# Two groups of weight sums moved to VectorE and the next batch's x sums moved one quad later, in a fused FFT mixing and ELU feed-forward kernel

## The chip, the cores and the metric

The kernel runs on one core of a Trainium2 chip. The metric is the time of one execution in microseconds (us) on the device; lower is better. A core has TensorE (PE, matrix multiply), VectorE (DVE), ScalarE (ACT), GpSimd (POOL) and SyncE (SP). In this kernel SP does nothing but issue DMA transfers, one after the other; a few transfers are issued by POOL and ACT. Each engine runs its own instructions in program order and waits on semaphores of the others.

## The reference

Two stages, all in float32. The first multiplies each of 8 sequences of length 3008 (256 channels) by a filter in the frequency domain; the second is a feed-forward block with an ELU between two matrix products.

```python
X = np.fft.rfft(x, axis=1)                 # x: (8, 3008, 256)
F = (filt_r + 1j * filt_i)[None, :, :]     # 1505 frequencies x 256
y = np.fft.irfft(X * F, n=3008, axis=1)
h = y.reshape(24064, 256) @ w_in           # 256 x 2048
g = np.where(h > 0.0, h, np.exp(np.minimum(h, 0.0)) - 1.0)
out = g @ w_out                            # 2048 x 256
```

## The kernel before

**The transform.** 3008 is 47 x 64. Each of the 8 batches goes through a transform along 64 (a_unit on PE, from x sums made by x_unit on DVE), a transform along 47 with the filter between (b_unit, then the products and sums re_mult, re_sums, im_mult, im_join, im_sums on DVE, then bi_unit), and a transform back along 64 (n_unit). Between these steps the data goes through DRAM to change its layout: z_write and z_read between a_unit and b_unit, y_write and y_read between bi_unit and n_unit. For the first batch there are separate functions (names with `_first`) that run in a prologue.

**The feed-forward block.** The result of n_unit for a batch and a sixth m (448 tokens for m=0, 512 for the others) is the input of four items q = 0 to 3, one for each quarter of the 2048 hidden columns. Both products use a Strassen scheme with seven products in place of eight, so for each item there are seven "up" steps (w_in) and seven "down" steps (w_out), each of four matmuls. An up step's result is kept by ACT (`keep`, L552) or added by DVE (`add`, L549); the ELU takes two ACT operations (`elu_exp`, L558 and L559) and one of DVE (`elu_max`, L563), and four more DVE operations make the combinations for the down steps (L599 to L603). The scheme also needs sums of pieces of the weights: `w_sums(k)` makes four of them, each 128x256, for piece k. The 16 weight pieces arrive as float64 and are converted on the chip: `w_split` (DVE), `w_float` (four ACT operations), `w_join` (DVE), then `w_sums` for every second piece.

**Quads.** The main loop (L977) runs over quads: quad i holds the seven up steps of item i and the seven down steps of item i-1, interleaved in a fixed order. For i from 0 on, item i is (b, m, q) in order, six times four items, so 24 quads, to a batch. All other work is put into a plan, `plan[(quad, place)]`, a list of functions for four places in a quad: places 2 and 3 come after the third and fifth step of the first half, place 0 in the middle, place 1 at the end of the quad. A list is run in the order in which `at(quad, place, fn, ...)` filled it:

```python
for fn, a in plan.get((i, 0), ()):
    fn(*a)
```

The table of the weight pieces fills it first, then f_pairs and the clearings, then the loop `for b in range(B)` with everything of batch 0, then everything of batch 1, and so on. In the loop for batch b, t is (b-1)*24. The order inside a quad, and the position of each engine's and each queue's instructions, follows from this alone; there is no other scheduler.

The quads of batch 0 up to quad 7 in the profiled execution, by the start of their first step on PE:

| quad | starts at (us) | what stands at its end on PE before the change |
|---|---|---|
| 0 | 87.0 | |
| 1 | 94.3 | n_unit(0,1), 106.03 |
| 2 | 107.8 | a_unit(1,0), 124.14 |
| 3 | 126.6 | a_unit(1,2), 137.44 |
| 4 | 139.3 | a_unit(1,4), 150.86 |
| 5 | 152.8 | n_unit(0,2), 164.94 |
| 6 | 166.7 | b_unit(1,0), 178.91 |
| 7 | 183.2 | |

**SP's queue.** x_load(b, c) issues seven transfers (one of the table ta, six of x), z_write(b, c) two (L308), z_read(b, g) four (L314), tn_read and y_read one each (L471, L477), f_pairs(c, u) three or four (L775 to L779), y_write four, and o_unit the out writes of a sixth, 24 for m=0 (L672, the DVE part being two adds and the transposes at L662). x_load for chunk c+4 can only start when a_unit has freed the buffer of chunk c.

**Where POOL works.** POOL issues the filter reads (f_read, L324), and before the change makes the sums of pieces 7, 11 and 13 (L750) and clears two filter buffers (L933).

Of the kernel before, what the change touches and what calls it, by code (L numbers as in the profile page):

```python
# [131 lines left out]
def kernel(  # L132
# [9 lines left out]
    nc = tc.nc  # L142
# [34 lines left out]
    fbufs = [fall[:, i] for i in range(FBUFS)]  # L177
# [502 lines left out]
    def w_fetch(k, queue=nc.gpsimd):  # L680
        q, j = divmod(k, 4)

        if k in (3, 4, 14, 15):
            wd = t2[:, k % 11 - 3].rearrange("p u d -> p (u d)")
        elif k == 10:
            wd = t1p.tile([P, XC, D], FP32, tag="t1", name="wd").rearrange("p u d -> p (u d)")
        elif k in (6, 7, 8, 9):
            wd = xp.tile([P, 2, 2, D], FP32, tag="xc", name="wd").rearrange("p k u d -> p (k u d)")
        else:
            wd = fbufs[{5: 0, 11: 0, 12: 1, 13: 2}.get(k, k)].rearrange("p c u d -> p (c u d)")  # L690
        wd = wds[k] = wd.bitcast(U32).rearrange("p (a w) -> p a w", w=2)
        if j < 2:
            srcs = [moe_w_in.bitcast(U32)[ts(j, P), ts(q, 1024)]]
        else:
            srcs = [moe_w_out.bitcast(U32)[ts(4 * q + 2 * (j - 2) + i, P), :] for i in range(2)]
        for i, s in enumerate(srcs):
            n = 512 // len(srcs)
            queue.dma_start(wd[:, ts(i, n), :].rearrange("p a w -> p (a w)"), s)
# [6 lines left out]
    def w_split(k):  # L705
        m, e, f, l = wts[k] = wtmp[{9: 2, 10: 1, 11: 0, 12: 3, 13: 4, 15: 5}.get(k, k % 2)]
        hi = wds[k][:, :, 1]
        nc.vector.tensor_scalar(out=m, in0=hi, scalar1=0x000FFFFF, scalar2=None, op0=ALU.bitwise_and)
        nc.vector.tensor_scalar(out=e, in0=hi, scalar1=0x7FF00000, scalar2=None, op0=ALU.bitwise_and)

    def w_float(k, *parts):
        m, e, f, l = wts[k]
        ef = e.bitcast(FP32)
        steps = ((l, wds[k][:, :, 0], AXT.Identity, 2.0 ** -52, 0.0), (f, m, AXT.Identity, 2.0 ** -20, 1.0),
                 (ef, e, AXT.Relu, -8.0, edges[:, 0:1]), (e, ef, AXT.Relu, -1.0, edges[:, 1:2]))
        for i in parts or range(4):
            o, x, func, scale, bias = steps[i]
            nc.scalar.activation(out=o, in_=x, func=func, scale=scale, bias=bias)

    def w_join(k, parts=(0, 1)):  # L720
        q, j = divmod(k, 4)
        m, e, f, l = wts[k]
        if 0 in parts:
            nc.vector.scalar_tensor_tensor(out=e, in0=wds.pop(k)[:, :, 1], scalar=0x80000000, in1=e,
                                           op0=ALU.bitwise_and, op1=ALU.bitwise_or)
            nc.vector.tensor_tensor(out=f, in0=f, in1=l, op=ALU.add)
        if 1 not in parts:
            return
        e = e.bitcast(FP32)
        if j < 2:  # L730
            f, e = (t.rearrange("p (a j c) -> p a j c", a=2, j=2) for t in (f, e))
            dst = w_in[q][:, 2 * j:2 * j + 2, :, :].rearrange("p j a c -> p a j c")
            nc.vector.tensor_tensor(out=dst, in0=f, in1=e, op=ALU.mult)
        else:

            f, e = (t.rearrange("p (i a e s) -> p i e a s", i=2, a=4, e=2) for t in (f, e))
            dst = w_out[q][:, 0:4, j - 2, :].rearrange("p (i e) (a s) -> p i e a s", i=2, a=4)
            for i in range(2):
                nc.vector.tensor_tensor(out=dst[:, i], in0=f[:, i], in1=e[:, i], op=ALU.mult)
        if j % 2 == 1 and k < 7:  # L740
            w_sums(k)

    def w_sums(k, engine=nc.vector, parts=(0, 1, 2, 3)):
        q, j = divmod(k, 4)
        w = (w_in if j < 2 else w_out)[q]
        a11, a21, a12, a22, s1, s2, s4 = (w[:, i] for i in range(7))
        sums = ((s1, a21, a22, ALU.add), (s2, s1, a11, ALU.subtract), (s4, a12, s2, ALU.subtract), (a21, a11, a21, ALU.subtract))
        for i in parts:
            o, x, y, op = sums[i]
            engine.tensor_tensor(out=o, in0=x, in1=y, op=op)  # L750
# [30 lines left out]
    with tc.manual_schedule():  # L781


        with tc.tile_pool(name="boot", bufs=1) as bp:
# [68 lines left out]
            c = t1p.tile([P, XC, D], FP32, tag="t1", name="wfl").rearrange("p (a b) d -> p a (b d)", a=2)  # L853
            places(c[:, 0], flat(tnp.tile([P, 4, P], FP32, tag="tn", name="we")), c)
            for t in (zq, rq):
                t = t.rearrange("p a u d -> p a (u d)")
                places(t[:, 0], t[:, 1], t[:, 2:4])
            t = t3f.rearrange("p a (b u) d -> p (a b) (u d)", u=2)
# [1 line left out]
            w_split(7)  # L860
            w_join(6)
            w_split(8)
            floats = {0: (7, 0, 1), 1: (7, 2, 3), 2: (8, 0, 1), 3: (8, 2, 3), 4: (9, 0, 1), 5: (9, 2, 3), 6: (10, 0, 1), 7: (10, 2, 3)}
            for g in range(4):
                t_first(g)
            for g in range(NG + 2):
# [20 lines left out]
            y_read(0, 0, slice(0, K2 - 4), slice(K2 - 4, K2))  # L887
            for k in (14, 15):
                w_fetch(k, nc.sync)
            w_join(8)  # L890
            for k in (11, 12, 13):
                w_split(k)
# [2 lines left out]
            w_sums(9)  # L895
            w_join(10)
            w_join(11)
            w_sums(11, nc.gpsimd)
            warm = psO.tile([P, 512], FP32, tag="po2", name="warm")
            for k in range(7):  # L900
                nc.tensor.matmul(warm, w_in[0][:, 0, 0, :], w_in[0][:, 0:2].rearrange("p a b c -> p (a b c)"),
# [15 lines left out]
        def at(quad, place, fn, *a):  # L917
            plan.setdefault((quad, place), []).append((fn, a))


        for quad, place, fn, *a in ((0, 0, w_split, 14), (1, 2, w_join, 12), (1, 2, w_split, 15), (1, 2, w_float, 14, 0, 1),
                                    (1, 3, w_float, 14, 2, 3), (2, 2, w_float, 15, 0, 1), (2, 3, w_float, 15, 2, 3),
                                    (2, 0, w_join, 14, (0,)), (2, 1, w_join, 14, (1,)), (2, 1, w_join, 15),
                                    (3, 0, w_sums, 15, nc.vector, (0, 1, 2)), (3, 1, w_sums, 15, nc.vector, (3,))):
            at(quad, place, fn, *a)
        for c in range(2, XBUFS):
# [3 lines left out]
            for u in range(2):  # L930
                at(1 + 2 * c + u, 0, f_pairs, c, u)
        for i in range(2):
            at(2 + i, 1, nc.gpsimd.memset, fbufs[i], 0.0)  # L933
        for b in range(B):
            t = (b - 1) * PER
            if b > 0:
                for c, s in enumerate((2, 2, 3, 3, 4, 4) if b == 1 else (0, 0, 3, 3, 4, 4)):
                    at(t + s, 0, x_unit, b, c)
                    if c % 2 == 0:
                        opens.add(t + s + 1)  # L940
                        at(t + s, 1, a_unit, b, c)
                    nb, nxt = (b, c + XBUFS) if c + XBUFS < NXC else (b + 1, c + XBUFS - NXC)
                    if nb < B:
                        at(t + s, 1, x_load, nb, nxt)
                    at(t + s, 1, z_write, b, c)
                for g in range(0, NG, 2):
                    s = t + 6 + 2 * g
                    opens.update((s + 1, s + 4))
                    for k in (g, g + 1):
                        at(s - 2, 1, f_read, b, k)  # L950
                        at(s - 1, 0, z_read, b, k)
                    at(s, 1, b_unit, b, g)
                    at(s + 1, 2, re_mult, b, g)
                    at(s + 1, 1, re_sums, b, g)
                    parts = ((0, 0), (0, 1), (1, 0), (1, 1))
                    early = 3 if g == 6 else 4
                    at(s + 2, 2, im_mult, b, g, *parts[:early])
                    at(s + 2, 1, im_mult, b, g, *parts[early:])
                    at(s + 2, 1, im_join, b, g)
                    at(s + 3, 2, im_sums, b, g)  # L960
                    at(s + 3, 1, bi_unit, b, g)
                    at(s + 3, 1, y_write, b, g)
            for m, (s, place) in enumerate(((23, 0), (25, 1), (29, 1), (32, 0), (36, 0), (40, 0))):
                if b > 0 or m > 0:
                    at(t + s - 2, 0, tn_read, b, m)
                    at(t + s - 2, 1 if m == 0 else 0, y_read, b, m)
                    at(t + s, place, n_unit, b, m)

                    at(*((t + s + 1, 1) if m > 2 else (t + s, place)), n_sums, b, m)
                if b == 0 and m == 1:  # L970
                    at(1, 1, w_join, 13)
                    at(1, 1, w_sums, 13, nc.gpsimd)
                at(t + PER + 4 * m + 5, 0, c_unit, b, m)
                at(t + PER + 4 * m + 6, 0, o_unit, b, m)

        items = [(b, m, q) for b in range(B) for m in range(6) for q in range(4)]
        for i in range(-PER, len(items) + 3):  # L977
# [3 lines left out]
            for n, k in enumerate("DUUDUDDU" if i in opens else "UUDUDDU"):  # L981
                s = ups if k == "U" else downs
# [7 lines left out]
            for k in "DUUDUD" if i in opens else "DUUDUDD":  # L990
                s = ups if k == "U" else downs
# [40 lines left out]
```

## Time and profile before

Three executions took 2587.74, 2592.74 and 2596.02 us; the median is 2592.74. The profiled execution took 2593.74 us, of which the span of the instructions is 2591.9.

| | |
|---|---|
| median of three executions | 2592.74 us |
| profiled execution, its span | 2593.74 us, 2591.9 us |
| PE busy | 2551.7 us, 98% of the span |
| DVE busy | 2041.2 us, 79% |
| ACT busy | 1548.1 us, 60% |
| POOL busy | 169.1 us, 7% |
| mean granted clock of PE | 0.993 |

How to read the lines. A timeline line has the start, the time (of one instruction or, merged, of a run of them), engine, source line, operation, the tile written and the tiles read, the shape, and in brackets how long the engine had been idle before and what ended that. SPq is SP's sequencer, which issues transfers. A line of waits names the engine and line that waited, what it waited for, and the total, the count and the longest wait in us. A row of a stretch (`A:B`) has its length, the busy time of PE, PE's weight loads, DVE, ACT and POOL with instruction counts, the granted clock of PE as a share of full speed, the busy share of the DMA engines, and GB/s.

### The profile page before, as it was taken

The page shows a single profiled execution, that of the slowest core. Times are in us where ns is not written, and L with a number is a line of the kernel's source. Part 1 is how long each engine was busy: PE and PEld are TensorE (multiplying, and loading weights), DVE is VectorE, ACT ScalarE, POOL GpSimd, SP SyncE. Part 2 cuts the span into 40 slices and gives each one's busy share as a digit, 9 for nine tenths or more (in the row PEclk, how much of TensorE's full clock was granted, in tenths as well). Part 3 has the DMA queues.
Part 4 walks back from the last instruction along what each step waited for, and adds up shares of the span by engine and source line. Part 5 has one row for each costly group of instructions (what it writes and reads, how often), then busy time and mean ns, then how long its engine had stood idle before and what let it go on. Part 6 is the DMA issues. An engine that isn't in the chain of part 4 may idle for free.

```text
span 2591.9 us, 39471 instructions
## 1 busy us (share of the span) xinstructions
PE 2551.7 (98%) x14474; PEld 2204.0 (85%) x14474; DVE 2041.2 (79%) x3524; ACT 1548.1 (60%) x2713; POOL 169.1 (7%) x325
## 2 busy tenths in 40 slices
PE   6899999999999999999999999999999999999998
PEld 4688889888898888988889888888889888898887
DVE  6868887788877888788886888778887788866666
ACT  6755556656566655665556656566655655555554
POOL 5100100010000000000000000000000010000000
PEclk8999999999999999999999999999999999999999
DMA  9662213422234231433215231243213322110010
GB/s 282 169 184 69 70 36 88 129 70 63 51 100 108 61 78 42 119 81 76 62 44 151 63 84 37 78 122 84 61 43 87 91 60 68 37 49 20 21 29 17
DMA packets 229177, 206.35 MB, mean 80 GB/s; under 512 B 128666, under 2 KB 195418, under 8 KB 228984
## 3 DMA queue, kind: packets, MB, share of 16 engines
q1 hardware_dynamic: 213624, 172.94, 26.2%
q0 software_dynamic: 14000, 30.44, 4.3%
q8 instruction: 114, 1.87, 0.3%
q10 hardware_dynamic: 1360, 0.46, 0.1%
q14 instruction: 79, 0.65, 0.1%
HBM read 131.87 MB, written 78.17 MB: 81 GB/s over the span
## 4 chain that ended last, share of the span: by engine, by line
PE 96%; DMA 2%; DVE 1%; ACT 0%; issue 0%; SPq 0%; DVEq 0%; ACTq 0%
PE po L623 44%; PE phs L541 25%; PE phd L541 13%; PE pha L541 6%; PE psn L490 3%; PE psa L234 2%; PE pf L383 2%; PE pv L455 1%; DMA xc<-in_x_dram 1%; DMA x<-in_x_dram 0%; PE po L330 0%; DMA yd<-t 0%; PE po L296 0%; PE psr L330 0%; DMA t<-yd 0%
## 5 line engine op out<-in xcount | busy, mean ns | idle before, releaser
L623 PE MATMUL po<-g,wo 128*128 128x256 f32 (+1 forms) x5376 | 1315.1, 377 | 0.0
L623 PEld LDWEIGHTS po<-g,wo 128*128 128x128 f32 x5376 | 1013.6, 190 | 163.6 <-issue 49.7
L552 ACT ACTIVATE g<-phs 128x512 f32<-128x512 f32 (+1 forms) x576 | 339.0, 589 | 751.6 <-PE phs L541 750.2
L559 ACT ACTIVATE e<-e 128x512 f32<-128x512 f32 (+1 forms) x768 | 477.2, 621 | 24.4
L549 DVE TENSOR_TENSOR g<-phd,g 128x512 f32<-128x512 f32 (+1 forms) x384 | 259.6, 676 | 293.6 <-ACT e L559 205.1
L541 PE MATMUL phs<-ys,wi 128*128 128x256 f32 (+1 forms) x1536 | 387.6, 375 | 2.0 <-ACT g L552 1.5
L541 PE MATMUL phs<-y,wi 128*128 128x256 f32 (+1 forms) x1536 | 388.5, 375 | 0.0
L563 DVE SCALAR_TENSOR_TENSOR g<-e,g 128x512 f32<-128x512 f32 (+1 forms) x576 | 387.3, 672 | 0.3 <-ACT e L559 0.2
L558 ACT ACTIVATE e<-g 128x512 f32<-128x512 f32 (+1 forms) x576 | 353.4, 614 | 46.7 <-DVE g L549 38.1
L541 PEld LDWEIGHTS phs<-ys,wi 128*128 128x128 f32 x1536 | 291.4, 190 | 36.0 <-ACT g L552 3.0
L541 PEld LDWEIGHTS phs<-y,wi 128*128 128x128 f32 x1536 | 288.2, 190 | 35.8 <-ACT g L552 0.2
L563 DVE SCALAR_TENSOR_TENSOR g<-e,phs 128x512 f32<-128x512 f32 (+1 forms) x192 | 130.0, 677 | 140.3 <-ACT e L559 139.9
L541 PE MATMUL phd<-ys,wi 128*128 128x256 f32 (+1 forms) x768 | 196.2, 378 | 3.1 <-DVE g L549 3.1
L541 PE MATMUL pha<-y,wi 128*128 128x256 f32 (+1 forms) x768 | 194.0, 375 | 0.0
L541 PE MATMUL phd<-y,wi 128*128 128x256 f32 (+1 forms) x768 | 193.7, 375 | 0.0
L558 ACT ACTIVATE e<-phs 128x512 f32<-128x512 f32 (+1 forms) x192 | 113.0, 589 | 128.7 <-PE phs L541 128.7
L541 PEld LDWEIGHTS phd<-ys,wi 128*128 128x128 f32 x768 | 145.0, 191 | 24.1 <-DVE g L549 8.2
L541 PEld LDWEIGHTS pha<-y,wi 128*128 128x128 f32 x768 | 145.6, 190 | 17.5 <-ACT y L492 0.2
L541 PEld LDWEIGHTS phd<-y,wi 128*128 128x128 f32 x768 | 145.8, 190 | 16.5
L324 POOL DMA_DIRECT2D fall<-fp x224 | 110.5, 501 | 733.4 <-DVE r L428 704.3
L549 DVE TENSOR_TENSOR g<-pha,g 128x512 f32<-128x512 f32 (+1 forms) x192 | 129.3, 673 | 25.9 <-PE pha L541 25.7
L600 DVE TENSOR_TENSOR g<-g,g 128x512 f32<-128x512 f32 (+1 forms) x192 | 130.7, 681 | 6.6
(155 smaller groups left out, 2097.8 us busy)
## 6 DMA issues: line engine op xcount, KB each, us to landing
yd<-t SPq DMA_DIRECT2D x127, 192.0 KB
t<-yd SPq DMA_DIRECT2D x47, 512.0 KB
z<-t SPq DMA_DIRECT2D x84, 256.0 KB
fall<-fp POOLq DMA_DIRECT2D x224, 96.0 KB, 3.0
t<-z SPq DMA_DIRECT2D x224, 96.0 KB
out_dram<-o SPq DMA_DIRECT2D x632, 32.0 KB
tn<-tn_t SPq DMA_DIRECT2D x48, 256.0 KB
xc<-in_x_dram SPq DMA_DIRECT2D x84, 128.0 KB
```

Of the source, the lines that this page charges most:

```text
L234: nc.tensor.matmul(p[o:o + 64, u, :], w[r, u, o:o + 64], src[r, u, :], start=True, stop=True)
L324: nc.gpsimd.dma_start(t[32 * a:32 * a + 24].rearrange("p c u d -> p (c u d)"), fp[g, a].rearrange("q c u d -> q (c u d)"))
L383: nc.tensor.matmul(pf[p][1][32 * a:32 * a + 32, js, :], fb[r, v, :], t2[r, js, a, :], start=True, stop=True, tile_position=(32 * p, 32 * a))
L490: nc.tensor.matmul(ps[:, ts(q, P)], t[:, i - 4 * m, ds(dh * P, P)], w[:, i - 4 * m, :], start=True, stop=True)
L541: nc.tensor.matmul(ps[:, a, 0:h], w_in[q][:, COMBO[n], a, :], y[n], start=start and a == 0, stop=True, skip_group_check=True)
L549: nc.vector.tensor_tensor(out=g[o], in0=i0, in1=i1, op=ALU.add)
L552: nc.scalar.activation(out=g[o], in_=i0, func=AXT.Copy)
L558: nc.scalar.activation(out=e, in_=src, func=AXT.Relu, scale=-1.0)
L559: nc.scalar.activation(out=e, in_=e, func=AXT.Exp, scale=-1.0)
L563: nc.vector.scalar_tensor_tensor(out=g[n], in0=es[n], scalar=1.0, in1=src, op0=ALU.subtract, op1=ALU.max)
L600: nc.vector.tensor_tensor(out=b12, in0=b22, in1=b12, op=ALU.subtract)
L623: nc.tensor.matmul(po[i][:, u, 0:h], w_out[q][:, COMBO[n], a, :], g[n][:, a, :], start=q == 0 and a == 0 and n in (1, 3, 6, 4), stop=True, ...
```

## The change

Seven small edits of the plan and of the prologue:

- The last two conversions of piece 10 are issued after the loop over the spectrum groups, no longer in its group 7.
- The four sums of piece 11 move from POOL, at the prologue's end, to DVE in the middle of quad 0, behind `w_split(14)`.
- The four sums of piece 13 move from POOL, at the end of quad 1, to DVE in quad 2, place 2. The first part of `w_join(14)` moves from the middle of quad 2 to place 2 as well, behind these sums.
- The clearings of the two filter buffers move from POOL (ends of quads 2 and 3) to ACT (both in quad 3, places 2 and 3).
- For batch 1 the x sums, with a_unit, the x loads and the z writes behind them, move from quads 2, 3 and 4 to quads 3, 4 and 5. The quads whose order of steps opens with a down step move along.
- The z reads of batch 1, g = 0 and 1, move from the middle of quad 5 to the middle of quad 6.
- n_unit(0,2) moves from the end of quad 5 to the middle of quad 4, with its tn and y reads from quad 3 to quad 2; its sums stay at the end of quad 5.

In the list of (quad 6, place 0) the out writes and the reads of batch 0 are entered in the loop's turn for b = 0, the z reads in its turn for b = 1.

```diff
--- before.py
+++ after.py
@@ -860,7 +860,7 @@
             w_split(7)
             w_join(6)
             w_split(8)
-            floats = {0: (7, 0, 1), 1: (7, 2, 3), 2: (8, 0, 1), 3: (8, 2, 3), 4: (9, 0, 1), 5: (9, 2, 3), 6: (10, 0, 1), 7: (10, 2, 3)}
+            floats = {0: (7, 0, 1), 1: (7, 2, 3), 2: (8, 0, 1), 3: (8, 2, 3), 4: (9, 0, 1), 5: (9, 2, 3), 6: (10, 0, 1)}
             for g in range(4):
                 t_first(g)
             for g in range(NG + 2):
@@ -887,6 +887,7 @@
             y_read(0, 0, slice(0, K2 - 4), slice(K2 - 4, K2))
             for k in (14, 15):
                 w_fetch(k, nc.sync)
+            w_float(10, 2, 3)
             w_join(8)
             for k in (11, 12, 13):
                 w_split(k)
@@ -895,7 +896,6 @@
             w_sums(9)
             w_join(10)
             w_join(11)
-            w_sums(11, nc.gpsimd)
             warm = psO.tile([P, 512], FP32, tag="po2", name="warm")
             for k in range(7):
                 nc.tensor.matmul(warm, w_in[0][:, 0, 0, :], w_in[0][:, 0:2].rearrange("p a b c -> p (a b c)"),
@@ -918,9 +918,9 @@
             plan.setdefault((quad, place), []).append((fn, a))
 
 
-        for quad, place, fn, *a in ((0, 0, w_split, 14), (1, 2, w_join, 12), (1, 2, w_split, 15), (1, 2, w_float, 14, 0, 1),
+        for quad, place, fn, *a in ((0, 0, w_split, 14), (0, 0, w_sums, 11), (1, 2, w_join, 12), (1, 2, w_split, 15), (1, 2, w_float, 14, 0, 1),
                                     (1, 3, w_float, 14, 2, 3), (2, 2, w_float, 15, 0, 1), (2, 3, w_float, 15, 2, 3),
-                                    (2, 0, w_join, 14, (0,)), (2, 1, w_join, 14, (1,)), (2, 1, w_join, 15),
+                                    (2, 2, w_sums, 13), (2, 2, w_join, 14, (0,)), (2, 1, w_join, 14, (1,)), (2, 1, w_join, 15),
                                     (3, 0, w_sums, 15, nc.vector, (0, 1, 2)), (3, 1, w_sums, 15, nc.vector, (3,))):
             at(quad, place, fn, *a)
         for c in range(2, XBUFS):
@@ -930,11 +930,11 @@
             for u in range(2):
                 at(1 + 2 * c + u, 0, f_pairs, c, u)
         for i in range(2):
-            at(2 + i, 1, nc.gpsimd.memset, fbufs[i], 0.0)
+            at(3, 2 + i, nc.scalar.memzero, fbufs[i])
         for b in range(B):
             t = (b - 1) * PER
             if b > 0:
-                for c, s in enumerate((2, 2, 3, 3, 4, 4) if b == 1 else (0, 0, 3, 3, 4, 4)):
+                for c, s in enumerate((3, 3, 4, 4, 5, 5) if b == 1 else (0, 0, 3, 3, 4, 4)):
                     at(t + s, 0, x_unit, b, c)
                     if c % 2 == 0:
                         opens.add(t + s + 1)
@@ -948,7 +948,7 @@
                     opens.update((s + 1, s + 4))
                     for k in (g, g + 1):
                         at(s - 2, 1, f_read, b, k)
-                        at(s - 1, 0, z_read, b, k)
+                        at(s if b == 1 and g == 0 else s - 1, 0, z_read, b, k)
                     at(s, 1, b_unit, b, g)
                     at(s + 1, 2, re_mult, b, g)
                     at(s + 1, 1, re_sums, b, g)
@@ -960,16 +960,15 @@
                     at(s + 3, 2, im_sums, b, g)
                     at(s + 3, 1, bi_unit, b, g)
                     at(s + 3, 1, y_write, b, g)
-            for m, (s, place) in enumerate(((23, 0), (25, 1), (29, 1), (32, 0), (36, 0), (40, 0))):
+            for m, (s, place) in enumerate(((23, 0), (25, 1), (28, 0) if b == 0 else (29, 1), (32, 0), (36, 0), (40, 0))):
                 if b > 0 or m > 0:
                     at(t + s - 2, 0, tn_read, b, m)
                     at(t + s - 2, 1 if m == 0 else 0, y_read, b, m)
                     at(t + s, place, n_unit, b, m)
 
-                    at(*((t + s + 1, 1) if m > 2 else (t + s, place)), n_sums, b, m)
+                    at(*((t + s + 1, 1) if m > 2 or s == 28 else (t + s, place)), n_sums, b, m)
                 if b == 0 and m == 1:
                     at(1, 1, w_join, 13)
-                    at(1, 1, w_sums, 13, nc.gpsimd)
                 at(t + PER + 4 * m + 5, 0, c_unit, b, m)
                 at(t + PER + 4 * m + 6, 0, o_unit, b, m)
```

## The prediction

> **What bounds the kernel now.** I read the page's engine rows first, then TensorE's waits, then the timeline around the two places where it idles inside the batch loop, then the queue of SyncE (SP). From the page:
>
> ```profile
> PE 2551.7 (98%) x14474; PEld 2204.0 (85%) x14474; DVE 2041.2 (79%) x3524; ACT 1548.1 (60%) x2713; POOL 169.1 (7%) x325
> PEclk8999999999999999999999999999999999999999
> ```
>
> TensorE (PE) is busy for 98% and from about 190 us on it is never idle. So each microsecond won or lost on PE before that moves the end by as much, and nothing later gives it back. Only the first batch's start-up can change. The waits of PE:
>
> ```profile
> PE phd L541 <- DVE g L549: 3.1, 1, 3.1
> ```
>
> The place, in the timeline of quad 2:
>
> ```profile
> 112.77 4.13 POOL L750 TENSOR_TENSOR wi<-wi 128x256 f32<-128x256 f32 x4 [22.55 <-DVE wi L733]
> 113.97 1.21 DVE L726 TENSOR_TENSOR wfl<-wfl 128x512 f32<-128x512 f32 x1
> 115.10 1.21 DVE L220 TENSOR_TENSOR sd<-xc 128x512 f32<-128x512 f32 x1
> 116.35 1.10 DVE L221 TENSOR_TENSOR xc<-xc 128x512 f32<-128x512 f32 x1
> 117.37 0.68 DVE L220 TENSOR_TENSOR sd<-xc 128x512 f32<-128x512 f32 x1
> 118.69 0.62 DVE L549 TENSOR_TENSOR g<-phd,g 128x448 f32<-128x448 f32 x1
> 119.36 1.86 PE L541 MATMUL phd<-ys,wi 128*128 128x224 f32 x4 [3.06 <-DVE g L549]
> ```
>
> VectorE (DVE) must do two join operations and four x sums before the add at L549 that PE's last up step waits for. While POOL runs the sums of piece 13 beside it, the same 512-wide operation takes 1.1 to 1.2 us in place of 0.68. The granted clock (the column after POOL's) then halves:
>
> ```profile
> 82.95:85.05 2.10, 0.00 (x0) 0.00 (x0) 2.07 (x5) 2.07 (x5) 0.00 (x0) 1.00 0.89 170
> 118.80:125.80 7.00, 6.44 (x32) 4.93 (x36) 6.04 (x12) 2.31 (x4) 0.00 (x0) 0.53 0.00 0
> 183.70:186.90 3.20, 3.20 (x9) 2.51 (x8) 2.35 (x4) 1.92 (x7) 0.00 (x0) 0.50 0.18 32
> ```
>
> The second row is the price of the stall; the third follows the other weak place, b_unit(1,0) at 178.91, whose 40 matmuls took 4.34 us (1.72 in the next batch) because its z reads landed late. SP's queue there, and the same in the next batch:
>
> ```profile
> 170.81 1.72 SPq L308 DMA_DIRECT2D z<-t  x2
> 175.76 3.17 SPq L314 DMA_DIRECT2D t<-z  x8
> 179.29 11.15 SPq L672 DMA_DIRECT2D out_dram<-o  x24
> 190.49 0.42 SPq L471 DMA_DIRECT2D tn<-tn_t  x1
> 191.48 6.04 SPq L314 DMA_DIRECT2D t<-z  x8
> ```
>
> ```profile
> 478.87 1.24 SPq L308 DMA_DIRECT2D z<-t  x2
> 482.90 3.18 SPq L314 DMA_DIRECT2D t<-z  x8
> 489.65 12.18 SPq L672 DMA_DIRECT2D out_dram<-o  x24
> 502.87 4.55 SPq L314 DMA_DIRECT2D t<-z  x8
> ```
>
> The reader should see two things: SP issues in order, and 24 out writes keep it for 11 to 12 us. Today the first eight z reads stand ahead of these writes.
>
> **The change, part by part.** All against the profiled execution: 2593.74 us, span 2591.9, 1.8 around it. It is 1.0 above the median of 2592.74.
>
> *Piece 10's last two conversions after the spectrum loop.* They run on ScalarE (ACT) at 74.16 for 1.48 us, between the copies of bi_first(5) and bi_first(6). Those copies can come up to some 0.3 us sooner (PE feeds them). But ACT still has to finish all conversions before the first L492 copy at 86.31, ahead of which it idled only 0.74. I count 0, between +0.3 and -0.3.
>
> *Sums 11 from POOL to DVE.* Beside POOL's sums (86.42 to 89.64) L518 and L519 took 0.91 and 0.80, alone 0.42 each (109.79, 110.24). Quad 0 is a chain of such waits, so its first part gains 0.6 (taken; 0 to 0.9). The four sums cost DVE 1.68 (their row at 80.66) in a place where it idled 1.63, before 92.72. Hidden; without that gap they would delay the add of quad 0.
>
> *Sums 13 to DVE, x sums out of quad 2.* DVE from 113.05 (the b11 add at 112.51 over): four sums 1.68, two joins of piece 14 at 1.32 (57.63 to 58.95), the b22 add 0.62: done at 116.67. PE is ready for it at 116.30 (115.38 + 0.92). The stall shrinks from 3.06 to 0.4: -2.7. The half clock behind it goes too: from 119.36 to 126.64 PE did one up step, two down steps and a_unit, 4.16 at full clock (0.755 a step, 1.89), in 7.28: -3.1.
>
> *What is late next: quad 3.* In quad 2 PE no longer waits, and a_unit (1.9) goes as well; DVE loses the time in which it caught up. From 116.67 it owes nine 448-wide operations at 0.571 (seven took 4.00 from 121.26 to 125.26), 5.14; the rest of join 14, 0.67; join 15, 2.09; the b11 add 0.57; three sums of piece 15, 1.33; now the x sums, four at 0.665, 2.66; the b22 add 0.62. That is 13.08: done at 129.75. PE needs it 14 steps after its last start at 116.7, at 127.27. A new stall of +2.5 (0.5 to 3.5, for the walk's small idles). Does the clock fall for it? In the rows above 2.1 us of idling left it at 1.00, 3.06 halved it. I take no fall, and keep up to +3.4 for the range.
>
> [...]
>
> *Clearings on ACT, and the rest.* 128x4096 took ACT 3.62, so two of 128x1024 take 0.9 each; ACT idles 1.7 twice in that stretch (before 130.73 and 133.00). Zero. POOL's eight f reads stand behind a_unit's freed buffer in quad 4, but those rows went out at 163.8 today and serve quad 7. Factor m=2 in quad 4 is the same 1.78 of PE, with its two reads on SP in a stretch (110.8 to 126) where SP had nothing. The second f_pairs group falls into that stretch too, with its 3.3 us wait at L779. All zero; the cover is idle time.
>
> So PE reaches b_unit(1,0) at 178.91 - 0.6 - 2.7 - 3.1 + 2.5 = 175.0, and a_unit(1,4), now at quad 5's end, started 12.2 + 1.9 earlier, at 160.9.
>
> *The z reads one quad later.* They move to the middle of quad 6, where the plan's list already holds o_unit(0,0) (24 out writes) and the tn and y reads of m=3, entered there in the turn of batch 0. The reads are appended behind them, and SP issues in that order. The chain: from a_unit's start to the last z write is issued, 12.1 (467.96 to 480.11; 780.84 to 792.78 gives 11.9); from the first out write to the eighth z read behind it 17.8 (489.65 to 507.42; 17.7 and 18.2 in batches 3 and 1); from there to b_unit's end 4.25 (178.93 to 183.18). 160.9 + 12.1 + 17.8 + 4.25 = 195.05, against 183.18: +11.9. PE, in order, stands some 18 us before b_unit, with quad 7 queued behind it; DVE and ACT starve with it.
>
> *Clock after it.* The clock is half for certain. Today's late b_unit already paid 1.6 (3.2 us at half); now part of the 40 matmuls is at half clock (up to 1.7 more) and the low stretch may last 7.0 (1.9 more). I take +1.1, between 0 and 3.4.
>
> Sum: +11.9 + 1.1 = +13.0: 2606.7 in this execution's terms, 2605.7 against the median.
>
> **The rivals.**
> A, the reads don't queue behind the out writes (not slower). If SP took them first, the z write's completion is the only wait: 173.0, then 2.8 (480.11 to 482.90), 3.2 and 4.25 give b_unit's end at 183.2, no change at all: 2592.7. For: today's order has them first. Against: the list of quad 6. To become faster the eighth read would have to be issued by 172.5, before the last z write has even gone. It decides only if the reads precede all 24 writes; each write ahead costs 0.47.
> B, DVE decides more: the stall of quad 2 stays in part, or quad 3's takes the clock with it. a_unit(1,4), from which SP's chain hangs, comes 3 to 6 later, and all behind it: 2609 to 2614. For: DVE's 13.08 us of owed work against 10.57. Against: a 2.5 us stall is under the 3.06 that halved the clock.
> C, quad 3 stalls little, since DVE finds shorter gaps: +8 to +10, 2601 to 2603.
> D, all is hidden: PE reaches b_unit at 175.0, its late 2.6 and its clock 1.6 go: -8.1, 2584.6. It needs SP 18 us earlier; no row has that.
>
> **How the numbers follow.** My forecast (2603 to 2609) 0.55, B 0.17, C 0.14, A 0.10, D 0.04. A measurement tells about 0.3% (7.8 us) from no change: slower means above 2600.5. Faster 0.04 (D), same 0.12 (A and the low edge of C), slower 0.84. The range leaves out A, D and the top of B: 2600 to 2613. The ends of the unknowns together reach from +8 to +22, but seldom at once.
>
> **What would show it.** In the profile after: no 3 us wait of phd at quad 2, and POOL without L750 after 62 us; a wait of phd on L549 in quad 3 of 1 to 3 us; on SP, the 24 out writes first, then tn, y and eight z reads; a PE wait for z of 15 to 19 us before pf, and a half clock behind it. I am wrong if the reads go out first, if SP's 17.8 us shrink, or if DVE's walk is off by more than a few operations.

## The result and the profile after

The changed kernel takes 2608.2 us (median of six executions, 2607.09 to 2608.93) against 2592.55 for the kernel before (six, 2587.74 to 2596.02): a ratio of 1.006, 95% interval 1.0047 to 1.0073. It is slower by some 15 us. The profiled execution took 2607.36 us, 13.6 more than that of before.

From the page of the kernel after, the engines and the chain that ended last by engine:

```profile
PE 2549.8 (98%) x14474; PEld 2202.7 (85%) x14474; DVE 2040.3 (78%) x3532; ACT 1549.6 (59%) x2715; POOL 159.3 (6%) x315
PE 95%; DMA 2%; DVE 1%; SPq 1%; issue 0%; ACT 0%; DVEq 0%; ACTq 0%
```

The busy times are the same to 0.2% but for POOL's sums and clearings; nothing has become dearer by itself. New is SPq in the chain: 1% of the span, where it had 0%. SP's issuing of transfers is now a part of the chain that sets the end. The waits of PE after the change say for what:

```profile
PE pf L383 <- DMA t<-z: 15.7, 1, 15.7
PE phd L541 <- DVE g L549: 2.3, 2, 2.1
```

The second line answers to the 3.1 us wait of before: it has moved and shrunk. The first is new. The timeline of DVE and PE shows the second:

```profile
112.90 1.67 DVE L750 TENSOR_TENSOR wi<-wi 128x256 f32<-128x256 f32 x4
115.69 0.61 DVE L549 TENSOR_TENSOR g<-phd,g 128x448 f32<-128x448 f32 x1
116.36 1.02 PE L541 MATMUL phd<-ys,wi 128*128 128x224 f32 x4 [0.21 <-DVE g L549]
124.75 1.33 DVE L750 TENSOR_TENSOR wo<-wo 128x256 f32<-128x256 f32 x3
128.05 0.69 DVE L221 TENSOR_TENSOR xc<-xc 128x512 f32<-128x512 f32 x1
128.66 0.62 DVE L549 TENSOR_TENSOR g<-phd,g 128x448 f32<-128x448 f32 x1
129.33 1.02 PE L541 MATMUL phd<-ys,wi 128*128 128x224 f32 x4 [2.11 <-DVE g L549]
```

In quad 2 PE waits 0.21 us in place of 3.06. In quad 3 the b22 add stands behind three sums of piece 15 and the four x sums, and PE waits 2.11. The matmuls after it keep their 1.02 us: the clock did not fall. Up to here the change wins what it was made of. Then SP's queue, and PE at b_unit(1,0):

```profile
172.49 1.26 SPq L308 DMA_DIRECT2D z<-t  x2
174.10 11.92 SPq L672 DMA_DIRECT2D out_dram<-o  x24
186.07 0.42 SPq L471 DMA_DIRECT2D tn<-tn_t  x1
186.54 0.43 SPq L477 DMA_DIRECT2D t<-yd  x1
187.01 12.81 SPq L314 DMA_DIRECT2D t<-z  x16
```

```profile
174.40 1.03 PE L623 MATMUL po<-g,wo 128*128 128x256 f32 x4
191.15 5.44 PE L383 MATMUL pf<-t,pairs 24*32 24x256 f32 x40 [15.72 <-DMA t<-z]
196.52 2.07 PE L623 MATMUL po<-g,wo 128*128 128x256 f32 x4
```

SP issues in order here: the first z read goes out 12.9 us after the first out write. PE's last down step of quad 6 starts at 174.40 and ends at about 175.3; b_unit ends at 196.5. The granted clock (the third number from the right in these rows of stretches) is half for 20 us:

```profile
180.70:200.90 20.20, 9.76 (x50) 5.04 (x51) 2.66 (x4) 2.69 (x8) 0.00 (x0) 0.50 0.45 123
200.90:204.00 3.10, 3.10 (x16) 2.73 (x15) 2.39 (x4) 1.57 (x3) 0.00 (x0) 1.00 0.15 40
```

Half of that stretch PE idles anyway; from 191 to 201 it pays for it.

### The profile page after: what moved, and what is told of

Same layout as the page of the kernel before. It is cut to its first block, busy times and chain, and to the rows that moved or that the text cites. A ratio compares the mean times of both kernels' runs of the same rounds, so it can differ in the third digit from the quotient of the medians.

```text
span 2605.6 us, 39458 instructions
## 1 busy us (share of the span) xinstructions
PE 2549.8 (98%) x14474; PEld 2202.7 (85%) x14474; DVE 2040.3 (78%) x3532; ACT 1549.6 (59%) x2715; POOL 159.3 (6%) x315
## 4 chain that ended last, share of the span: by engine, by line
PE 95%; DMA 2%; DVE 1%; SPq 1%; issue 0%; ACT 0%; DVEq 0%; ACTq 0%
PE po L623 43%; PE phs L541 25%; PE phd L541 12%; PE pha L541 6%; PE psn L490 3%; PE pf L383 2%; PE psa L234 1%; PE pv L455 1%; DMA xc<-in_x_dram 1%; PE po L330 1%; DMA x<-in_x_dram 0%; SPq L672 0%; PE po L296 0%; PE psr L330 0%; DVE g L549 0%
```

## The experiments

The start-up before the loop ends at a different time in each run: the first up step starts between 85.8 and 90.0 us, whatever the edit. So next to the medians the table gives a stretch within the profiled execution, from the first matmul of the first up step to the first of n_unit(0,3), which lies behind b_unit(1,0). Behind it no wait of PE is listed in the kernels before and after (PE is busy for 2380.5 of the 2387.0 us from 203 on and for 2393.2 of the 2396.0 from 204 on), so the stretch holds all that the change can move, but for the prologue. It is that of one execution each, and a half clock behind a stall alone moves it by up to 2.9 us (see the last section), so small differences are read from its parts.

| kernel | median us, before beside it | ratio, 95% interval | stretch, us | wait of phd in quads 2 and 3 |
|---|---|---|---|---|
| before | 2592.55 | | 116.14 | 3.06, 0 |
| after | 2608.20, 2592.55 | 1.0060, 1.0047 to 1.0073 | 129.51 | 0.21, 2.11 |
| late_reads_alone | 2607.93, 2593.68 | 1.0048, 1.0033 to 1.0063 | 129.01 | 3.07, 0 |
| reads_first | 2595.84, 2593.68 | 1.0005, 0.9995 to 1.0014 | 116.52 | 0.21, 2.12 |
| tn_last | 2606.37, 2592.47 | 1.0053, 1.0039 to 1.0067 | 126.87 | 0.21, 2.12 |
| sums_alone | 2591.96, 2593.68 | 0.9994, 0.9984 to 1.0004 | 115.58 | 2.87, 0 |
| writes_first | 2586.66, 2593.68 | 0.9973, 0.9961 to 0.9984 | 108.50 | 0.21, 2.11 |
| wf_sums13_pool | 2587.06, 2592.47 | 0.9972, 0.9959 to 0.9984 | 108.06 | 0, 2.20 |
| wf_float_back | 2590.58 (one execution) | | 110.84 | 0.22, 2.12 |
| wf_sums15_late | 2585.13, 2592.47 | 0.9973, 0.9959 to 0.9986 | 108.15 | 0.21, 0.87 |
| wf_sums15_again | 2585.97, 2593.35 | 0.9978, 0.9969 to 0.9987 | 107.23 | 0.22, 0.87 |
| before_writes_first | 2588.82, 2593.35 | 0.9987, 0.9978 to 0.9996 | 109.69 | 3.07, 0 |
| wf_all_pool | 2585.78, 2593.35 | 0.9970, 0.9961 to 0.9980 | 107.31 | 0, 0.95 |

### Is it SP's order? The z reads ahead of the out writes, and the z reads late alone

reads_first takes the kernel after and puts the z reads at the head of the list of quad 6, place 0:

```diff
-                        at(s if b == 1 and g == 0 else s - 1, 0, z_read, b, k)
+                        if b == 1 and g == 0:
+                            plan.setdefault((s, 0), []).insert(k, (z_read, (b, k)))
+                        else:
+                            at(s - 1, 0, z_read, b, k)
```

> The changed kernel with one thing altered: in the middle of quad 6 the eight z reads of batch 1 stand ahead of the 24 out writes. Theory (SP's order is the price): the last z write goes out at about 173.7 as after the change, the first z read 2.8 later, the eighth by 179.8, and b_unit(1,0) ends near 184 in place of 196.5. PE still idles some 6 to 7 us before it, so the clock halves: 2593 to 2597, which is 12 to 14 below the changed kernel. Rival (the x sums and a_unit one quad later are the price, not the order behind the out writes): b_unit(1,0) ends at 193 or later, 2604 to 2609.

late_reads_alone takes the kernel before and makes the one change that puts the reads behind the out writes:

```diff
-                        at(s - 1, 0, z_read, b, k)
+                        at(s if b == 1 and g == 0 else s - 1, 0, z_read, b, k)
```

> The kernel before with one thing altered: the eight z reads of batch 1, g = 0 and 1, are issued in the middle of quad 6, behind the out writes; nothing else of the change. Theory (SP's order is the price): out writes from about 173, b_unit(1,0) ends 22 later, near 195, 12 later than before: 2603 to 2607. Rival (the late z reads are only dear because a_unit(1,4) is a quad later): the z writes are out at 172.5 already, b_unit ends before 188: 2592 to 2598.

SP's queue, and below it PE at b_unit, in reads_first:

```profile
171.89 1.25 SPq L308 DMA_DIRECT2D z<-t  x2
175.90 3.17 SPq L314 DMA_DIRECT2D t<-z  x8
179.44 11.14 SPq L672 DMA_DIRECT2D out_dram<-o  x24
178.37 5.64 PE L383 MATMUL pf<-t,pairs 24*32 24x256 f32 x40 [3.50 <-DMA t<-z]
```

and in late_reads_alone, with PE's wait from the view of waits:

```profile
173.53 2.09 SPq L308 DMA_DIRECT2D z<-t  x2
175.97 11.51 SPq L672 DMA_DIRECT2D out_dram<-o  x24
188.47 5.01 SPq L314 DMA_DIRECT2D t<-z  x8
```

```profile
PE pf L383 <- DMA t<-z: 11.3, 1, 11.3
```

One line moved in each, and the loss goes and comes. With the reads first the stretch falls from 129.5 to 116.5, no longer to be told from before. With the reads late alone the kernel before becomes as slow as the kernel after (stretch +12.9 of the change's +13.4). The rival, that the x sums and a_unit one quad later are the price, is out: reads_first has them all. reads_first is also the rival A of the prediction, made true, and it gave "no change", as worked out there: b_unit ended at 183.93, foreseen 183.2. Two details of the expectations were off. PE waited 3.5 us before b_unit in reads_first, not 6 to 7. And late_reads_alone came out 1 us above its range; its out writes began 3 us later than expected, but its first up step began 3.1 us later than that of the kernel before (90.04 for 86.96).

### What the late reads are made of

tn_last leaves the z reads behind the 24 writes but takes them before the tn and y reads of m=3:

```diff
-                    at(t + s - 2, 0, tn_read, b, m)
-                    at(t + s - 2, 1 if m == 0 else 0, y_read, b, m)
+                    if (b, m) != (0, 3):
+                        at(t + s - 2, 0, tn_read, b, m)
+                        at(t + s - 2, 1 if m == 0 else 0, y_read, b, m)
...
                         at(s if b == 1 and g == 0 else s - 1, 0, z_read, b, k)
+                        if (b, k) == (1, 1):
+                            at(s, 0, tn_read, 0, 3)
+                            at(s, 0, y_read, 0, 3)
```

> The changed kernel with one thing altered: in the middle of quad 6 the tn and y reads of m=3 stand behind the eight z reads, which still follow the 24 out writes. It prices the two parts of the 17.8 us chain. Theory (of the 17.8, some 12 are the writes and the rest the reads, of which 1.0 is the issue of tn and y and about 2 the eighth z read's wait for the y read): b_unit(1,0) ends 2 to 3 sooner relative to the first out write, 2605 to 2607. Rival (the z reads are held by the out writes' own landing, not by SP's issue): no difference, 2607 to 2609.

SP's queue and PE in tn_last:

```profile
172.86 11.92 SPq L672 DMA_DIRECT2D out_dram<-o  x24
184.83 3.23 SPq L314 DMA_DIRECT2D t<-z  x8
187.35 6.30 PE L383 MATMUL pf<-t,pairs 24*32 24x256 f32 x40 [13.14 <-DMA t<-z]
```

From the first out write to b_unit's end it takes 20.7 us (172.86 to 193.58) in place of 22.4 (174.10 to 196.52): 1.7 sooner, a little less than expected. The stretch is 2.6 shorter; the other 0.9 is a shorter half clock behind b_unit. The eight reads went out in 3.2 us without the wait for y. So the writes' issue is the large part, tn and y the small one. The rival, that the writes' own landing holds the reads back, can be told from the same rows: b_unit's first matmul starts 2.52 us after the first z read is issued (184.83 to 187.35), and in reads_first, where no out write stands ahead, 2.47 (175.90 to 178.37). With the tn and y reads ahead, in the kernel after, it is 4.14 (187.01 to 191.15).

### Is it POOL, or DVE's total work? The sums alone

sums_alone is the kernel before with only the sums of 11 and 13 on DVE and the clearings on ACT:

```diff
-            w_sums(11, nc.gpsimd)
...
-((0, 0, w_split, 14), (1, 2, w_join, 12),
+((0, 0, w_split, 14), (0, 0, w_sums, 11), (1, 2, w_join, 12),
...
-(2, 0, w_join, 14, (0,)),
+(2, 2, w_sums, 13), (2, 2, w_join, 14, (0,)),
...
-        at(2 + i, 1, nc.gpsimd.memset, fbufs[i], 0.0)
+        at(3, 2 + i, nc.scalar.memzero, fbufs[i])
...
-                    at(1, 1, w_sums, 13, nc.gpsimd)
```

> The kernel before with the sums of pieces 11 and 13 on DVE (and the first part of join 14 behind them) and the clearings on ACT; x sums, z reads, n_unit and piece 10 as before. Theory (DVE's total work ahead of the b22 add of quad 2 sets the stall, and 1.7 us of sums on DVE cost as much as POOL's slowing of its neighbours): phd still waits on L549 for 2.4 to 3.1 us in quad 2, the clock halves behind it, 2590 to 2593. Rival (it is POOL beside DVE that makes the stall): the wait is under 1 us and the time 2586 to 2588.

DVE in quad 2 of sums_alone:

```profile
111.58 1.67 DVE L750 TENSOR_TENSOR wi<-wi 128x256 f32<-128x256 f32 x4
114.37 0.69 DVE L220 TENSOR_TENSOR sd<-xc 128x512 f32<-128x512 f32 x1
116.42 0.69 DVE L221 TENSOR_TENSOR xc<-xc 128x512 f32<-128x512 f32 x1
117.03 0.62 DVE L549 TENSOR_TENSOR g<-phd,g 128x448 f32<-128x448 f32 x1
```

No operation is slowed any more, and PE still waits 2.87 us. The 1.6 us of sums that DVE now does itself cost what POOL's neighbourhood had cost (four operations, two of join 14 and two x sums, at 1.0 to 1.2 in place of 0.69, together 1.8). The cure of quad 2 is the x sums' going, not the sums' coming. The reverse says the same: wf_sums13_pool is writes_first (below) with sums 13 back on POOL.

```diff
-(2, 2, w_sums, 13), (2, 2, w_join, 14, (0,)),
+(2, 2, w_join, 14, (0,)),
...
+                    at(1, 1, w_sums, 13, nc.gpsimd)
```

> The kernel writes_first with the four sums of piece 13 on POOL again, as before the change; x sums stay in quads 3 to 5. Theory (moving the x sums out of quad 2 cured its stall, the move of sums 13 to DVE did not): DVE's two joins take 1.0 and 1.2 beside POOL in place of 1.2 with 1.6 of sums ahead, so no wait over 0.4 in quad 2; the wait in quad 3 is 1.4 to 2.6, as DVE owes the same. 2584 to 2588, no measurable difference from writes_first. Rival (POOL beside DVE is what stalls PE): a wait of over 2 us in quad 2 or over 2.9 in quad 3 with a half clock, 2589 to 2593.

```profile
112.27 0.99 DVE L724 SCALAR_TENSOR_TENSOR we<-t,we 128x512 uint32<-128x512 uint32 x1
113.18 1.22 DVE L726 TENSOR_TENSOR wfl<-wfl 128x512 f32<-128x512 f32 x1
114.32 0.61 DVE L549 TENSOR_TENSOR g<-phd,g 128x448 f32<-128x448 f32 x1
```

The two joins are slowed to 0.99 and 1.22 and the add still starts in time: no wait of phd in quad 2, 2.20 in quad 3, the same time. wf_all_pool goes further: it is wf_sums15_late (below) with both groups of sums and the clearings back on POOL.

> The kernel wf_sums15_late with the sums of pieces 11 and 13 and the clearings back on POOL; the x sums one quad later, the early n_unit and SP's altered order stay. Theory (the cure of quad 2 is the x sums' going, and the sums on DVE are worth only the 0.6 us of quad 0): the stretch from the first up step to n_unit(0,3) is 0.3 to 1.2 longer than in wf_sums15_late, no wait over 0.5 in quad 2, 2584 to 2588. Rival (POOL's sums beside DVE are the cause of the stall): a wait of 1.5 us or more in quad 2 and a half clock, the stretch 3 us longer or more.

Its stretch is 107.31 against 107.23, its ratio to before the same. Quad 0 has lost its gain (L518 at 0.91 again, a 0.4 us wait of phs on it), quad 2 its last 0.2 us of waiting. The 0.3 to 1.2 us expected did not come: 0.08. So the moves of the sums and clearings to other engines are worth nothing that these runs can tell. No run moves the x sums or n_unit(0,2) alone; that the x sums' going is the cure follows from these runs together.

### A version that beats both

writes_first keeps the change and alters SP's order at the end of quad 5: both z writes, then the z reads, and the two x loads a quad later.

```diff
-                        at(t + s, 1, x_load, nb, nxt)
+                        at(t + s + (1 if b == 1 and c > 3 else 0), 1, x_load, nb, nxt)
...
-                        at(s if b == 1 and g == 0 else s - 1, 0, z_read, b, k)
+                        at(s - 1, 1 if b == 1 and g == 0 else 0, z_read, b, k)
```

> The changed kernel with SP's order altered at the end of quad 5: both z writes of a_unit(1,4), then the eight z reads, and the x loads that stood between the z writes only at the end of quad 6. Theory: the z writes go out at 164 to 166, the z reads from 169 to 172, all before PE reaches b_unit(1,0) near 175.3. No wait there and no half clock: 2583 to 2587, 6 to 9 below the kernel before. Rival (z writes and reads take longer than their issue, or the x loads are missed later): a wait of over 2 us before b_unit, 2590 or more.

SP's queue and PE in writes_first:

```profile
162.04 3.20 SPq L308 DMA_DIRECT2D z<-t  x4
168.16 3.17 SPq L314 DMA_DIRECT2D t<-z  x8
172.07 11.28 SPq L672 DMA_DIRECT2D out_dram<-o  x24
```

```profile
173.79 2.00 PE L383 MATMUL pf<-t,pairs 24*32 24x256 f32 x40
175.72 1.13 PE L623 MATMUL po<-g,wo 128*128 128x256 f32 x4
```

b_unit starts without a wait and takes 2.0 us, and the steps behind it run at full clock (1.00 granted from 172 to 180 us). 2586.66 us is 7.0 below the kernel before, at a ratio of 0.9973. The x loads are not missed: PE waits for nothing after b_unit. The same order works on the kernel before:

```diff
-                        at(s - 1, 0, z_read, b, k)
+                        at(s - 2 if b == 1 and g == 0 else s - 1, 1 if b == 1 and g == 0 else 0, z_read, b, k)
...
-                        at(t + s, 1, x_load, nb, nxt)
+                        at(t + s + (1 if b == 1 and c > 3 else 0), 1, x_load, nb, nxt)
```

> The kernel before with SP's order alone altered at the end of quad 4: both z writes of a_unit(1,4) and the eight z reads ahead of the two x loads, which go to the end of quad 5. Theory (the late z reads at b_unit are worth their 2.6 us of waiting and 1.7 of half clock): b_unit(1,0) takes 1.7 to 2.0 us in place of 4.3, the stretch from the first up step to n_unit(0,3) shrinks by 4 to 4.5 from 116.1, 2587 to 2590. Rival (PE waits for something else there): below 2 us of change in that stretch.

2588.82, a ratio of 0.9987. From b_unit's start to n_unit(0,3) it takes 19.9 us (176.17 to 196.07) in place of 24.2 (178.91 to 203.10): the 4.3 expected. The other 2.2 of the stretch's 6.5 are not the edit's: in quad 2 of this execution the clock did not fall (see the last section), which spared 2.9 us (4.36 in place of 7.28 from the last up step to the first step after a_unit), and some 0.7 was lost elsewhere.

wf_sums15_late takes the wait of quad 3 on: all four sums of piece 15 at the quad's end.

```diff
-(3, 0, w_sums, 15, nc.vector, (0, 1, 2)), (3, 1, w_sums, 15, nc.vector, (3,))
+(3, 1, w_sums, 15)
```

> The kernel writes_first with all four sums of piece 15 at the end of quad 3; before, three of them stood in its middle, ahead of the b22 add that PE waits for. Theory (the wait in quad 3 is DVE's queue of owed work): the 2.1 us wait shrinks by the three sums' 1.3 to 0.6 to 1.0, 2584 to 2587, about 1.3 below writes_first. Rival (the down steps of quad 4 need the sums sooner): a new wait of 0.5 us or more on po in quad 4 eats it.

> The kernel wf_sums15_late again, in more rounds, as the candidate that beats both kernels. Theory: from the first up step to n_unit(0,3) 107 to 108 us at full clock (116.1 before the change, 129.5 after it, 108.5 in writes_first), so 2583 to 2586. Rival (nothing is left to gain there): no difference from writes_first, 2586 to 2588.

The wait fell from 2.11 to 0.87, by 1.24 of the 1.3 expected, with no new wait on po. The first run's stretch of 108.15 began at half clock (its first up step took 1.70 us in place of 1.02); the second, at full clock, has 107.23, 1.3 below writes_first. In the medians, 2585.13 and 2585.97, this gain is below what they can tell from 2586.66.

### The prologue's edit

wf_float_back is writes_first with piece 10's last two conversions back in group 7 of the spectrum loop.

```diff
-5: (9, 2, 3), 6: (10, 0, 1)}
+5: (9, 2, 3), 6: (10, 0, 1), 7: (10, 2, 3)}
...
-            w_float(10, 2, 3)
```

> The kernel writes_first with piece 10's last two conversions back in group 7 of the spectrum loop. The start-up varies from run to run by more than this can move, so it is read within the trace. Theory (the moved conversions make ACT late for the first L492 copy): the 0.36 to 1.0 us wait of phs on ACT's y at the first up step, in all three kernels with this edit and in none without it, is gone, and the distance from the first psn matmul to the first phs matmul is 1.9 us in place of 2.4 to 3.0. Rival (the wait comes with the time at which the y read lands): the wait stays above 0.3.

The wait of phs on ACT's y is gone here, but this execution's start-up stalled 3.3 us before its first psn matmul and ran on at half clock (the first up step took 1.70 us, 1.02 in writes_first), so the distance asked for (2.57 us) says nothing. The count over all kernels says little more: of the eight with the edit six show the wait, 0.2 to 1.1 us, and of the five without it none does. But within the eight the wait shrinks as PE's stall before its first psn matmul grows: 1.0 and 1.1 us of wait at stalls of 1.2 and 1.4, 0.4 at 2.1, 0.2 at 2.3, none at 2.5 and 3.2 (the last at half clock). The five without the edit all stalled 2.15 us or more, so the time at which the y read lands is not ruled out as the cause. At like stalls (reads_first 2.06 with the edit, the kernel before 2.15 without) the wait is 0.36 against none, and ACT had idled 0.74 in the latter. That the edit costs some tenths of a microsecond is likely, not shown; the start-up varies by four.

## Why the prediction was right

2605.7 was forecast, 2600 to 2613 as the range, and 2608.2 measured. By its own steps, against the profile after:

- **Piece 10: 0.** Not quite. bi_first(7)'s copy came 0.04 sooner (76.46 for 76.50), since PE's matmuls fed it, and ACT was then 0.5 late for L492 (86.80 for 86.31). The first up step began 0.4 later; how much of that is the edit's stays open (see above).
- **Quad 0: -0.6.** From the first up step to n_unit(0,1) 18.51 in place of 19.07: -0.56.
- **Quad 2: a stall of 0.4 and no half clock.** 0.21, and the clock stayed at 1.00. But only the x sums' going has a share in it; taking POOL away has none, as wf_all_pool shows. The half clock, priced at 3.1, is worth 2.9 by before_writes_first.
- **Quad 3: a new stall of 2.5 without a half clock.** 2.11: DVE's walk from add to add was 12.97 (115.69 to 128.66), foreseen 13.08. That the clock stayed whole was in part luck: the same stall, 2.12, halved it in wf_float_back (see the last section). The 3.4 that the forecast kept as the dearest fall, here and behind b_unit, is shown by no run; behind a stall of these quads a fall cost 1.7 (wf_float_back) and 2.9 (quad 2 of the kernel before), and behind b_unit the three steps lost the 0.4 below.
- **PE reaches b_unit at 175.0.** 175.3, a down step of 0.86 from 174.40.
- **The z reads behind the out writes.** Last z writes at 173.0 foreseen, 173.75 measured; from the first out write to b_unit's end 22.05 foreseen, 22.42 measured; b_unit's end 195.05 foreseen, 196.52 measured. The sum had the first out write follow the last z write at once; it came 0.35 later.
- **The clock behind it: +1.1.** The three steps after b_unit took 4.82 in place of 4.38, +0.4, and b_unit's own half clock (a matmul of it took 1.06 us at the median, in the kernel before 0.59) lies in its end above.
- **Sum: +13.0.** The stretch says +13.4, the profiled executions +13.6, the medians +15.7. The last two microseconds between profile and median lie in which executions were profiled (before 1.2 above its median, after 0.8 below); the start-up varies by more.

The step that decided was one that no engine's busy time shows: to read the plan in the order in which it is filled, and to let SP issue one transfer after the other. What counted is the sum of the issues. Here 24 writes of 8 to 24 KB kept SP 11.9 us, half a microsecond each, and with the tn and y reads behind them they put the eight reads that PE waited for 12.9 us later in the queue.

## What to carry to other kernels

When a step moves by one place in a plan, look up what already stands in the new place, on the queues too: transfers that nobody waits for, issued ahead of one that PE waits for, can cost their whole issue time (here 11.9 us for the out writes and 0.9 for tn and y, with a loss of 13). A gain ahead of a handover (here PE reaches b_unit some 4 us sooner, counted from its first up step) is kept only if the next handover, through DRAM and back, is as early; put its writes and reads ahead of prefetches and results in the queue. And before moving work off an engine that slows its neighbour, work out what the neighbour then does itself: here the two were about equal, 1.6 us of sums and 1.8 of slowing.

## What the runs showed of the hardware

In these runs the length of a stall did not settle whether the granted clock fell. Quads 2 and 3 have ten waits of PE for an add of 2.1 us or more. The up step behind the wait tells the clock: its four matmuls took 1.02 us where it stayed whole, 1.70 or 1.86 where it fell.

| kernel | quad | wait of phd, us | up step behind it, us |
|---|---|---|---|
| before_writes_first | 2 | 3.07 | 1.02 |
| late_reads_alone | 2 | 3.07 | 1.86 |
| before | 2 | 3.06 | 1.86 |
| sums_alone | 2 | 2.87 | 1.86 |
| wf_sums13_pool | 3 | 2.20 | 1.02 |
| wf_float_back | 3 | 2.12 | 1.70 |
| reads_first | 3 | 2.12 | 1.02 |
| tn_last | 3 | 2.12 | 1.02 |
| after | 3 | 2.11 | 1.02 |
| writes_first | 3 | 2.11 | 1.02 |

The rows behind the wait in before_writes_first, wf_float_back and the kernel after, in this order:

```profile
119.00:122.40 3.40, 3.40 (x32) 2.87 (x36) 3.27 (x6) 2.31 (x4) 0.00 (x0) 1.00 0.00 0
131.80:135.30 3.50, 3.47 (x10) 3.15 (x11) 2.74 (x5) 2.19 (x4) 0.00 (x0) 0.53 0.00 0
129.30:132.60 3.30, 3.27 (x28) 2.80 (x32) 3.17 (x6) 2.31 (x4) 0.00 (x0) 1.00 0.00 0
```

The time at half clock differed too. In the kernel before it was 6.83 us in quad 2 and 3.41 at b_unit(1,0); in the kernel after 20.48 at b_unit, with PE busy for 9.71 of them:

```profile
118.62:125.45 6.83, 6.09 (x24) 4.67 (x28) 5.87 (x12) 2.31 (x4) 0.06 (x1) 0.50 0.00 0
180.00:183.47 3.47, 3.46 (x37) 1.05 (x36) 1.96 (x4) 0.14 (x1) 0.00 (x0) 1.00 0.40 87
183.47:186.88 3.41, 3.41 (x9) 2.70 (x9) 2.33 (x4) 2.13 (x7) 0.00 (x0) 0.50 0.20 36
```

```profile
180.37:200.85 20.48, 9.71 (x50) 5.03 (x51) 2.66 (x4) 2.64 (x8) 0.00 (x0) 0.50 0.44 121
```

At b_unit the busy time of a row does not tell either: in the kernel before the clock fell at 183.47, behind a row that shows PE busy for 3.46 of 3.47 us. What decides whether the clock falls, and for how long, these runs do not show.

So the prediction's reading of its rows, no fall at 2.1 us of stall and a fall at 3.06, holds for those two stalls and for no more: 2.12 us was followed by a fall in wf_float_back, 3.07 by none in before_writes_first. Its "no fall" in quad 3 came true at 2.11 us, as in four of the five other stalls of 2.1 to 2.2. A stall of two to three microseconds is best priced with the half clock as a chance: here it cost 1.7 us in wf_float_back (against writes_first, from n_unit(0,1) to n_unit(0,2)) and 2.9 in quad 2 of the kernel before.
